# The o products of an attention kernel in tiles of 64 rows, in two banks held for a whole head group, with two visits a stretch

## The chip, the cores and the metric

One core of a Trainium2 chip. The metric is device time in microseconds of one execution. TensorE (PE) multiplies, its weight loads are shown apart as PEld; VectorE is DVE, ScalarE is ACT, GpSimd is POOL, and SyncE (SP) issues the DMAs. Matmul results land in PSUM, which has eight banks of 128 partitions x 512 fp32 values.

## The reference, cut to what matters

x is 2048 tokens x 640 channels, with 32 heads of 20 channels that share one key and one value head.

```python
q = heads(x @ wq); k = x @ wk; v = x @ wv
scores = einsum("bhqd,bkd->bhqk", q, k) * Dh ** -0.5
o = einsum("bhqk,bkd->bhqd", softmax(scores), v)
a = merge(o) @ wo
u = gelu(einsum("bsd,sf->bdf", layernorm(x), w1) + b1)   # over tokens, F = 1728
b = transpose(einsum("bdf,fs->bds", u, w2) + b2)
return g * a + (1 - g) * b                               # g = sigmoid(x . gate_w)
```

## The kernel before, in words

**Data.** Matrices are split into a high and a low part in a 32-bit type that TensorE takes in one pass; a product is then three matmuls (high x high, high x low, low x high). Most have a contraction of at most 64 rows and occupy one half of TensorE's array, 64 rows x 128 columns, so that two run side by side, one in each half. The probabilities `p` and the values `v_sb` are plain fp32, and each matmul on them shows as two passes in the trace.

**Attention.** A head group `n` is four heads by 512 queries; there are 32 (`NU`). A unit `u` is one head group and one block of 128 keys (`kb`), 512 in all. For a unit there are four scores (`qk`, line 677: two in each half of the array), each 128 keys x 512 queries for one head, in a PSUM bank of their own; ACT turns each into a tile `p` (line 686). The o product of a unit (line 788) multiplies `v_sb` (128 keys x 32 columns: 20 channels, and ones for the sum of the softmax) with each of the four `p`: four tiles of 128 rows x 32 columns, side by side, into the four quarters of one bank `o`. Row maxima are found ahead, from products of their own (`ms_next`, line 508) that DVE reduces (line 514).

**Order.** After a lead-in, a Python planner writes the order of instructions. The work is cut into 244 stretches: 84 of the first MLP layer (`b1_jobs`, line 1069), 128 of the second (`b2_jobs`, line 866) and 32 of the output projection (`a_jobs`, line 1005), whose accumulating matmuls go into one bank `g` and are called `fs` in `main`. In a stretch one half of the array runs scores and maxima (`xs`), the other the `fs` with a few scores and maxima before and after; halves change roles from stretch to stretch. `main` keeps a clock for each half (`lanes`) and a list of banks with the times at which they come free (`pool`, seven banks: three `ms`, three `s`, one `o`, which scores and maxima use too), and always writes the half that is free first. Each score or maximum counts 0.232 us (`X_US`), each of the `fs` 0.147 us (`F_US`).

At the end of each stretch comes one visit: the o products of two units in one go (`pv_group`, line 778), eight matmuls of 128 x 32 in a bank taken from `pool`. ACT copies the result out (line 797 or 800), and POOL adds it to the head group's sum (line 801); after the last block of keys the sum is scaled and stored in steps that `settle` spreads over later stretches.

Units 488 to 511 (`TAIL`) follow in blocks of their own, with the same `pv_group`, one unit at a time and summing in the bank.

Of the kernel before, what the change touches and what calls it, by code (L numbers as in the profile page):

```python
# [9 lines left out]
F32 = mybir.dt.float32  # L10
F32R = mybir.dt.float32r
AF = mybir.ActivationFunctionType
# [5 lines left out]
P = 128  # L18
S, D, H, DH, F = 2048, 640, 32, 20, 1728
NS = S // P  # L20
# [4 lines left out]
NB = 512  # L25
NQB = S // NB
NQ = H // 4
NU = NQB * NQ
PRO = 7
LEAD = 45  # L30
TAIL = 24
# [13 lines left out]
def mix_kernel(ctx: ExitStack, tc: tile.TileContext, A_x, A_wq, A_wk, A_wv, A_wo,  # L45
               B_x, B_w1, B_b1, B_w2, B_b2, gate_w, out):
    nc = tc.nc
    x = A_x[0]
# [17 lines left out]
    v_sb = const.tile([P, NS, 32], F32, name="v_sb")  # L66
# [109 lines left out]
    with tc.tile_pool(name="pa", bufs=1) as pa, \  # L176
# [236 lines left out]
        for sb in range(NQB):  # L413
# [11 lines left out]
            for m in range(DC):  # L425
# [3 lines left out]
                p = q_parts(m, ts)  # L429
# [37 lines left out]
    ev = ctx.enter_context(tc.tile_pool(name="ev", bufs=1))  # L467
# [7 lines left out]
    def bank_take():  # L475
        i = min(range(len(pool)), key=lambda j: pool[j][0])
        return pool.pop(i)[1]
# [170 lines left out]
    ptiles = {}  # L648
# [125 lines left out]

    otile, sums = [], [None]
    later = []

    def pv_group(us, keep=False):
        n, kb = units[us[0]]
        assert units[us[-1]][0] == n  # L780
        if not otile:
            otile.append(bank_take())
        o = otile[0]
        opened = not keep or kb == 0 or us[0] == len(units) - TAIL
        ends = kb + len(us) == NS
        for i, u in enumerate(us):
            for hh in range(4):
                nc.tensor.matmul(o[32 * hh:32 * hh + 32, :], v_sb[:, kb + i, :], ptiles.pop((u, hh)),  # L788
                                 start=opened and i == 0, stop=(i == len(us) - 1) and (ends or not keep),
                                 skip_group_check=True)  # L790
        if not keep:
            begin = max(clock["act"], clock["pv"] + 0.14)
            clock["act"] = begin + 0.477
            pool.append((begin + 0.65, otile.pop()))
            if kb == 0:
                sums[0] = ev.tile([P, NB], F32, name="acc", bufs=2)
                nc.scalar.activation(sums[0], o, AF.Copy)
            else:
                part = ev.tile([P, NB], F32, name="part", bufs=2)
                nc.scalar.activation(part, o, AF.Copy)  # L800
                nc.gpsimd.tensor_add(sums[0], sums[0], part)  # L801
        if ends and n < NU - 1:
            qb, g = divmod(n, NQ)
            ot = ev.tile([P, NB // 32, 32], F32, name="ot")
            rl = ev.tile([P, NB // 32], F32, name="rl")
            on = sums[0]
            flat = ot.rearrange("p c e -> p (c e)")
            oh, ol = flat.bitcast(F32R), on.bitcast(F32R)
            if keep:
                nc.vector.tensor_add(on, on, o)  # L810

            def turned():
                nc.vector.transpose(flat, on)
                nc.vector.reciprocal(rl, ot[:, :, DH])
                nc.vector.tensor_mul(ot, ot, rl[:, :, None].to_broadcast([P, NB // 32, 32]))

            def back():
                nc.vector.transpose(on, flat)

            def sums_out():  # L820
                for hh in range(4):
                    r = 32 * hh + DH
                    nc.sync.dma_start(out=l_scr[0, n, hh:hh + 1], in_=on[r:r + 1, :])

            def sums_in():
                nc.sync.dma_start(out=rl, in_=l_scr[0, n].rearrange("h (r c) -> (h r) c", r=32))

            def inverse():
                busy("dve", 0.17)
                nc.vector.reciprocal(rl, rl)  # L830
                nc.sync.dma_start(out=l_scr[1, n].rearrange("h (r c) -> (h r) c", r=32), in_=rl)

            def inverse_in():
                for hh in range(4):
                    nc.sync.dma_start(out=flat[32 * hh:32 * hh + 32, :],
                                      in_=l_scr[1, n, hh:hh + 1].to_broadcast([32, NB]))

            def scale():
                nc.gpsimd.tensor_mul(on, on, flat)

            def high():
                nc.gpsimd.tensor_copy(oh, on)

            def low():
                nc.gpsimd.tensor_sub(ol, on, f32(oh))
                for j, t in enumerate((oh, ol)):
                    for hh in range(4):
                        r = (4 * g + hh) * DH
                        nc.sync.dma_start(out=o_scr[j, r:r + DH, qb * NB:(qb + 1) * NB],
                                          in_=f32(t[32 * hh:32 * hh + DH, :]))  # L850

            first = (None, turned, back) if keep else (sums_out, sums_in, None, inverse, inverse_in, None, scale)
            later.extend((False, f) for f in (*first, high, low))
# [299 lines left out]

    lanes = [0.0, 0.0]
    fresh = [True, True]

    def issue(b, us, f, t):
        clock["now"] = max(t, clock["now"])
        f()
        lanes[b] = clock["now"] + us + (FIRST if fresh[b] else 0.0)  # L1160
        fresh[b] = False

    def main(k, vs, n_max):
        b = k % 2
        fs, rest, done = ph[k]
        fs, done = list(fs), list(done)
        known, kept = set(row_max), set(sent)
        end = 2 * ((vs[-1] if vs else -1) + 1)
        xs, side = pattern(k)
        before, after = side.split("F")  # L1170
        need = end + AHEAD - sc[b]
        if xs.count("s") < need:
            i = len(xs) * 2 // 3
            xs = xs[:i] + "s" * (need - xs.count("s")) + xs[i:]
        while xs.count("s") > need:
            i = xs.rindex("s")
            xs = xs[:i] + xs[i + 1:]
        if xs.count("m") < n_max[b]:
            xs += "m" * (n_max[b] - xs.count("m"))
        while xs.count("m") > n_max[b]:  # L1180
            i = xs.rindex("m")
            xs = xs[:i] + xs[i + 1:]
        after += "m" * (n_max[1 - b] - (before + after).count("m"))
        while (before + after).count("m") > n_max[1 - b]:
            if "m" in after:
                after = after.replace("m", "", 1)
            else:
                before = before.replace("m", "", 1)
        before = "s" * (end - sc[1 - b] - (before + after).count("s")) + before
        xs, before, after = list(xs), list(before), list(after)  # L1190
        total, count = len(xs) + len(before) + len(after) + len(fs), 0
        while fs or after or before or xs:
            if count == (total + 1) // 2:
                settle()
            count += 1
            free = min(e for e, _ in pool)
            tx = max(lanes[b], free) if xs else 1e9
            tf = 1e9
            if before or (after and not fs):
                tf = max(lanes[1 - b], free)  # L1200
            elif fs:
                tf = lanes[1 - b]
            if len(xs) == 1 and fs and not after:
                tx = 1e9
            if tf < tx or tf == tx and not before:
                if before or not fs:
                    c = (before or after).pop(0)
                    issue(1 - b, X_US, (s_next if c == "s" else ms_next)(1 - b) or (lambda: None), tf)
                else:
                    issue(1 - b, F_US, fs.pop(0), tf)  # L1210
                    while done and not fs:
                        done.pop(0)()
            else:
                c = xs.pop(0)
                issue(b, X_US, (s_next if c == "s" else ms_next)(b) or (lambda: None), tx)
        ms_done()
        spare[0] = len(row_max) == NU
        settle(len(vs) == 2)
        if vs:
            n, kb = units[vs[0]][0] + 1, units[vs[0]][1]  # L1220
            if n in kept and n in qtiles and n not in back_in:
                fetch_max(n)
                back_in.add(n)
        for f in rest:
            f()
        for i in sorted(known - sent):
            store_max(i)
            sent.add(i)
        if vs:
            start = max([max(lanes) + DRAIN, min(e for e, _ in pool)] + [ready[v] for v in vs])  # L1230
            clock["pv"] = start + len(vs) * PV_US + ENTER
            lanes[:] = [clock["pv"]] * 2
            fresh[:] = [True, True]
            pv_group(vs)

    ps_l.clear()
    in_lead.close()
# [5 lines left out]
    v = 0  # L1243
    clock.update(now=0.0, act=ACT_AT, dve=0.5, pv=0.0)
    for k in range(len(ph)):
# [5 lines left out]
        if k == len(ph) - 2:  # L1251
            w_last = split_last(raw)
    assert v == len(units) - TAIL
    spare[0] = True
    ring[:0] = extra_p

# [152 lines left out]
```

## Time and profile before

| | |
|---|---|
| median of 2 runs | 1608.35 us (1608.32 to 1608.38) |
| the profiled execution | 1608.27 us, its span 1606.5 us |
| granted TensorE clock | 1.00 |
| lead-in (projections, LayerNorm, first part of layer 1) | 0 to 161.8 us |
| 84 stretches with layer 1 | 161.8 to 662.3 us |
| 128 stretches with layer 2 | 662.3 to 1377.4 us |
| 32 stretches with the output projection | 1377.4 to 1532.2 us |
| the last 24 units and the end | 1532.2 to 1606.5 us |

The profile is one execution. A busy PE means that a matmul was under way, not that the array was full: matmuls overlap, and the distance from one start to the next says more than a duration. In a timeline row stand start, duration, engine, line, operation, output and inputs, then rows x columns of the array and the shape of the moving operand; several instructions of one kind that overlap are merged (x16).

### The profile page before, as it was taken

What the parts mean: (1) busy time and instruction counts of PE and PEld (TensorE: products, weight loads), DVE (VectorE), ACT (ScalarE), POOL (GpSimd) and SP (SyncE); (2) the same over time, 40 slices, a digit from 0 to 9 for tenths busy, and PEclk for the clock granted to TensorE, in tenths of its full rate; (3) what the DMA queues carried; (4) which work ended last, traced back from release to release, by engine and by line L of the source; (5) the groups of instructions that cost most, each with busy time, mean ns of one, the idle gap of its engine ahead of it and who ended that gap; (6) DMA issues with size and microseconds to landing.
All of it is one profiled execution on the core that took longest, in us unless ns stands there. A gap on an engine that the chain in (4) does not pass through costs nothing.

```text
span 1606.5 us, 39460 instructions
## 1 busy us (share of the span) xinstructions
PE 1600.9 (100%) x14864; PEld 1123.2 (70%) x14864; DVE 1355.0 (84%) x2301; ACT 1309.1 (81%) x2566; POOL 867.6 (54%) x976
## 2 busy tenths in 40 slices
PE   9999999999999999999999999999999999999999
PEld 7899677767776777666666666666666666666676
DVE  6689999999999999888888888888888888766644
ACT  4546888888888888888888888888888888999974
POOL 6568676768777687644544434454544333344420
PEclk9999999999999999999999999999999999999999
DMA  7655223323233323222222122222222112245521
GB/s 218 212 171 143 73 74 80 86 64 94 76 81 85 82 67 80 64 73 81 73 70 68 51 67 67 70 73 81 73 73 69 54 50 68 85 123 181 165 87 57
DMA packets 183750, 145.07 MB, mean 90 GB/s; under 512 B 38291, under 2 KB 145424, under 8 KB 183560
## 3 DMA queue, kind: packets, MB, share of 16 engines
q1 hardware_dynamic: 183272, 142.23, 31.4%
q8 instruction: 117, 1.92, 0.5%
q14 instruction: 73, 0.60, 0.1%
q10 hardware_dynamic: 288, 0.33, 0.1%
HBM read 108.75 MB, written 32.15 MB: 88 GB/s over the span
## 4 chain that ended last, share of the span: by engine, by line
PE 98%; DVE 1%; POOL 0%; ACT 0%; issue 0%; DVEq 0%; POOLq 0%
PE s L788 16%; PE ms L788 11%; PE g L866 11%; PE s L677 10%; PE g L1069 9%; PE ms L677 9%; PE ms L508 6%; PE s L508 6%; PE pp L307 4%; PE o L677 3%; PE o L508 2%; PE g L1005 2%; PE o L788 2%; PE s L720 1%; PE g L720 1%; PE s L960 1%
## 5 line engine op out<-in xcount | busy, mean ns | idle before, releaser
L514 DVE TENSOR_REDUCE mp<-ms 128x1 f32<-128x512 f32 x889 | 583.1, 682 | 79.8 <-PE ms L508 64.9
L686 ACT ACTIVATE p<-s 128x512 f32<-128x512 f32 x938 | 543.2, 617 | 39.6 <-PE ms L788 12.8
L514 DVE TENSOR_REDUCE mp<-s 128x1 f32<-128x512 f32 x759 | 503.2, 683 | 75.1 <-PE s L508 61.0
L686 ACT ACTIVATE p<-ms 128x512 f32<-128x512 f32 x808 | 471.9, 614 | 35.1 <-PE s L788 11.8
L801 POOL TENSOR_TENSOR acc<-acc,part 128x512 f32<-128x512 f32 x213 | 275.0, 1291 | 311.2 <-ACT part L800 300.8
L677 PE MATMUL s<-qst,kst 62*128 62x512 f32 x944 | 362.9, 407 | 0.0
L508 PE MATMUL ms<-kst,qmx 60*128 60x512 f32 x889 | 357.5, 416 | 0.0
L677 PE MATMUL ms<-qst,kst 62*128 62x512 f32 x810 | 319.1, 407 | 0.0
L1069 PE MATMUL g<-slot,wh 64*128 64x320 f32 x1344 | 306.1, 313 | 0.3 <-ACT p L686 0.3
L508 PE MATMUL s<-kst,qmx 60*128 60x512 f32 x759 | 304.0, 414 | 0.2 <-DVE mp L514 0.2
L788 PE MATMUL s<-p,v_sb 128*32 128x512 f32 x2240 | 269.3, 598 | 0.0
L1069 PEld LDWEIGHTS g<-slot,wh 64*128 64x128 f32 x1344 | 216.6, 185 | 70.1 <-issue 49.4
L134 POOL TENSOR_TENSOR wl<-wr,wh 128x512 fp32r<-128x512 f32 (+1 forms) x176 | 218.1, 1239 | 28.0 <-ACT wh L131 16.3
L514 DVE TENSOR_REDUCE mp<-o 128x1 f32<-128x512 f32 x308 | 210.1, 682 | 18.5 <-PE o L508 17.8
L677 PEld LDWEIGHTS s<-qst,kst 62*128 62x128 f32 x944 | 174.2, 185 | 59.1 <-ACT p L686 27.6
L1069 PE MATMUL g<-slot,wl 64*128 64x320 f32 x672 | 205.4, 306 | 0.0
L866 PE MATMUL g<-u,wh 64*128 64x320 f32 x864 | 196.5, 309 | 0.0
L866 PE MATMUL g<-slot,wh 64*128 64x320 f32 x864 | 196.4, 309 | 0.0
L677 PEld LDWEIGHTS ms<-qst,kst 62*128 62x128 f32 x810 | 150.0, 186 | 56.8 <-ACT p L686 28.3
L788 PE MATMUL ms<-p,v_sb 128*32 128x512 f32 x1560 | 189.4, 598 | 0.0
L686 ACT ACTIVATE p<-o 128x512 f32<-128x512 f32 x273 | 168.3, 617 | 12.7 <-PE ms L788 6.9
L508 PEld LDWEIGHTS ms<-kst,qmx 60*128 60x128 f32 x889 | 164.2, 185 | 3.6
(270 smaller groups left out, 3101.8 us busy)
## 6 DMA issues: line engine op xcount, KB each, us to landing
wr<-in_B_w_dram SPq DMA_DIRECT2D x136, 256.0 KB
qmx<-q_scr SPq DMA_DIRECT2D x192, 80.0 KB
qst<-q_scr SPq DMA_DIRECT2D x192, 80.0 KB
ot<-l_scr SPq DMA_DIRECT2D x120, 64.0 KB
y_scr<-yo SPq DMA_DIRECT2D x16, 320.0 KB
slot<-o_scr SPq DMA_DIRECT2D x16, 320.0 KB
o_scr<-ot SPq DMA_DIRECT2D x124, 40.0 KB
o_scr<-acc SPq DMA_DIRECT2D x124, 40.0 KB
```

What stands on the lines that cost most here:

```text
L134: nc.gpsimd.tensor_sub(wl[:, :nv], wr[:, :nv], f32(wh[:, :nv]))
L307: nc.tensor.matmul(pp, w, t, start=first and n == 0, stop=not more and n == len(steps) - 1)
L508: nc.tensor.matmul(ms, qmax[n][64 * b:64 * b + 60, pr, qt * P:(qt + 1) * P], kst[64 * b:64 * b + 60, kq * NB:(kq + 1) * NB], start=True, s ...
L514: r = nc.vector.tensor_reduce(mtiles[n][:, c, kq:kq + 1], ms, axis=AX.X, op=ALU.max)
L677: nc.tensor.matmul(s, kst[64 * b:64 * b + 62, kb * P:(kb + 1) * P], q[64 * b:64 * b + 62, pr, :], start=True, stop=True)
L686: e = nc.scalar.activation(p, s, AF.Exp, scale=SCALE)
L720: nc.tensor.matmul(pu[r][:, :HD2], w[rows, c, :], h[rows, st, :], start=(st == 0 and k == 0), stop=(st == NS - 1 and k == 2))
L788: nc.tensor.matmul(o[32 * hh:32 * hh + 32, :], v_sb[:, kb + i, :], ptiles.pop((u, hh)), start=opened and i == 0, stop=(i == len(us) - 1) a ...
L801: nc.gpsimd.tensor_add(sums[0], sums[0], part)
L866: other_tile(half, nc.tensor.matmul(hold["p"][:, :HD2], w[r, i, :], u[d][r, fc, :], start=(hold["n"] == 1), stop=(hold["n"] == 6 * FC - 3)))
L1005: other_tile(half, nc.tensor.matmul(hold["p"][:, :HD2], o[r, c, :], w[r, c, d * HD2:(d + 1) * HD2], start=(hold["n"] == 1), stop=(hold["n" ...
L1069: other_tile(half, nc.tensor.matmul(hold["p"][:, :HD2], w[r, st % HS, :], h[d][r, st, :], start=(hold["n"] == 1), stop=(hold["n"] == 6 * NS)))
```

## The change

Each o product becomes two, one for each half of the keys (64 rows x 32 columns), in the half of the array where these rows lie. Each half has an o bank of its own, which is taken at the first block of keys of a head group and given back after the last: the sum over the 16 blocks is now made in PSUM, and ACT and POOL add the two banks once (`o_out`). The four products of a unit in one half are written as two pairs (`o_pair`, `j` 0 and 1), as steps of that half's queue of work, counted 0.43 us each (`V_US`). Of the two units of a stretch, one has its place in the middle (at 0.5 of `xs`, at 0.6 of `fs`), the other at the end. The planner no longer lets both halves wait for each other around a visit. The list `waiting` stays empty. The last 24 units still use `pv_group`.

```diff
+    obank, used = {}, {}
+
+    def o_out(n, upto):
+        sums[0] = ev.tile([P, NB], F32, name="acc", bufs=2)
+        part = ev.tile([P, NB], F32, name="part", bufs=2)
+        for b, t in enumerate((sums[0], part)):
+            o = obank.pop((n, b))
+            begin = max(clock["act"], clock["now"] + 0.9)
+            clock["act"] = begin + 0.477
+            nc.scalar.activation(t, o, AF.Copy)
+            pool.append((begin + 0.65, o))
+        nc.gpsimd.tensor_add(sums[0], sums[0], part)
+        unit_end(n, upto)
+
+    def o_pair(u, b, j):
+        n, kb = units[u]
+        if (n, b) not in obank:
+            obank[n, b] = bank_take()
+        o, rows = obank[n, b], slice(64 * b, 64 * b + 64)
+        last = kb == NS - 1 or u == len(units) - TAIL - 1
+        for hh in (2 * j, 2 * j + 1):
+            nc.tensor.matmul(o[32 * hh:32 * hh + 32, :], v_sb[rows, kb, :], ptiles[u, hh][rows, :],
+                             start=kb == 0, stop=last, skip_group_check=True)
+        used[u] = used.get(u, 0) + 1
+        if used[u] == 4:
+            for hh in range(4):
+                ptiles.pop((u, hh))
+            if last:
+                o_out(n, kb + 1)
...
-        if not keep:
-            begin = max(clock["act"], clock["pv"] + 0.14)
-            clock["act"] = begin + 0.477
-            pool.append((begin + 0.65, otile.pop()))
-            if kb == 0:
-                sums[0] = ev.tile([P, NB], F32, name="acc", bufs=2)
-                nc.scalar.activation(sums[0], o, AF.Copy)
-            else:
-                part = ev.tile([P, NB], F32, name="part", bufs=2)
-                nc.scalar.activation(part, o, AF.Copy)
-                nc.gpsimd.tensor_add(sums[0], sums[0], part)
-        if ends and n < NU - 1:
+        unit_end(n, kb + len(us), keep, o)
+
+    def unit_end(n, upto, keep=False, o=None):
+        if upto == NS and n < NU - 1:
...
+    X_AT, F_AT, V_US = (0, 0.5, 1), (0, 0.6, 1), 0.43
...
+        def cut(items, places):
+            out, p = [], 0
+            for at, us in zip(places, [waiting, *([u] for u in vs)]):
+                n = round(at * len(items))
+                out += items[p:n] + [("v", (u, None, j)) for u in us for j in range(2)]
+                p = n
+            return out + items[p:]
+
+        xq = cut([("x", c) for c in xs], X_AT)
+        fq = [("x", c) for c in before] + cut([("f", f) for f in fs], F_AT) + [("x", c) for c in after]
...
+            h = 1 - b if tf < tx else b
+            kind, what = q[h].pop(0)
...
+            elif kind == "v":
+                issue(h, V_US, lambda: o_pair(what[0], h, what[2]), t)
...
-        if vs:
-            start = max([max(lanes) + DRAIN, min(e for e, _ in pool)] + [ready[v] for v in vs])
-            clock["pv"] = start + len(vs) * PV_US + ENTER
-            lanes[:] = [clock["pv"]] * 2
-            fresh[:] = [True, True]
-            pv_group(vs)
```

On TensorE, before, the end of one stretch in the second layer and the start of the next (`s`, `ms` and `o` are the rotating banks, whatever they hold; L677 scores, L508 products for maxima, L866 the layer's own matmuls, L788 o products):

```order
L866 MATMUL g<-slot_83,wh 128x320
L508 MATMUL ms<-kst,qmx 128x512
L866 MATMUL g<-slot_83,wl 128x320
L677 MATMUL s<-qst,kst 128x512
L788 MATMUL s<-p,v_sb 32x512 x8
L677 MATMUL s<-qst,kst 128x512
L508 MATMUL o<-kst,qmx 128x512
L866 MATMUL g<-slot_83,wh 128x320
```

All eight o products of two units stand together, and in the 37 rows of the stretch there is no other visit.

On TensorE, after, the middle of a stretch in the second layer (L887 is the line that was L866, L798 the new o products; `s` and `o` here are the two banks of the sums):

```order
L508 MATMUL s<-kst,qmx 128x512
L887 MATMUL g<-u_1163,wh 128x320
L798 MATMUL o<-p,v_sb 32x512 x2
L887 MATMUL g<-u_1163,wl 128x320
L798 MATMUL s<-p,v_sb 32x512 x2
L798 MATMUL o<-p,v_sb 32x512 x2
L798 MATMUL s<-p,v_sb 32x512 x2
L508 MATMUL s<-kst,qmx 128x512
L887 MATMUL g<-u_1163,wh 128x320
```

The eight products of one unit stand in the middle of the stretch, pair by pair in turn for the two halves, with one of the layer's matmuls between the first pair and the rest.

On TensorE, after, the end of the same stretch:

```order
L887 MATMUL g<-u_1163,wl 128x320
L798 MATMUL s<-p,v_sb 32x512 x2
L508 MATMUL ms<-kst,qmx 128x512
L798 MATMUL o<-p,v_sb 32x512 x2
L798 MATMUL s<-p,v_sb 32x512 x2
L798 MATMUL o<-p,v_sb 32x512 x2
L677 MATMUL ms<-qst,kst 128x512
```

The other unit's eight products, with a product for a maximum between the first pair and the rest.

More of the change, by code (lines that the diff above doesn't have):

```diff
@@ L1155, in mix_kernel @@
     fresh = [True, True]
+    waiting = []
+    X_AT, F_AT, V_US = (0, 0.5, 1), (0, 0.6, 1), 0.43
     def issue(b, us, f, t):
@@ L1189, in main, with at @@
         before = "s" * (end - sc[1 - b] - (before + after).count("s")) + before
-        xs, before, after = list(xs), list(before), list(after)
-        total, count = len(xs) + len(before) + len(after) + len(fs), 0
-        while fs or after or before or xs:
+        def cut(items, places):
[7 more added lines that the diff above has]
+        fq = [("x", c) for c in before] + cut([("f", f) for f in fs], F_AT) + [("x", c) for c in after]
+        waiting.clear()
+        q = {b: xq, 1 - b: fq}
+        n_f = len(fs)
+        total, count = len(xq) + len(fq), 0
+        def at(h):
+            if not q[h]:
+                return 1e9
+            kind, what = q[h][0]
+            if kind == "x":
+                return max(lanes[h], min(e for e, _ in pool))
+            if kind == "v":
+                u = what[0]
+                if any((u, i) not in ptiles for i in range(4)):
+                    return 1e8
+                t = max(lanes[h], ready[u] + 0.05)
+                return t if (units[u][0], h) in obank else max(t, min(e for e, _ in pool))
+            return lanes[h]
+        while xq or fq:
             if count == (total + 1) // 2:
@@ L1195, in main @@
             count += 1
[L1196 to L1203, printed above, removed]
-                tx = 1e9
[L1205 to L1212, printed above, removed]
-            else:
-                c = xs.pop(0)
-                issue(b, X_US, (s_next if c == "s" else ms_next)(b) or (lambda: None), tx)
+            tx, tf = at(b), at(1 - b)
+            if len(xq) == 1 and n_f and not after:
+                tx = 1e9
+            h = 1 - b if tf < tx else b
+            kind, what = q[h].pop(0)
+            t = min(tx, tf)
+            assert t < 1e8, (k, q)
+            if kind == "x":
+                issue(h, X_US, (s_next if what == "s" else ms_next)(h) or (lambda: None), t)
+            elif kind == "v":
+                issue(h, V_US, lambda: o_pair(what[0], h, what[2]), t)
+            else:
+                issue(h, F_US, what, t)
+                n_f -= 1
+                while done and not n_f:
+                    done.pop(0)()
         ms_done()
@@ L1253, in mix_kernel @@
     assert v == len(units) - TAIL
+    for u in waiting:
+        for j in range(2):
+            for h in range(2):
+                clock["now"] = lanes[h] = max(lanes[h], ready[u] + 0.05)
+                o_pair(u, h, j)
+                lanes[h] += V_US
+    lanes[:] = [max(lanes) + DRAIN] * 2
     spare[0] = True
```

## The prediction

> **What bounds the kernel now.** I read the page's busy times and the chain that ended last first, then the busy times of the stretches of the program, then single matmuls on TensorE's timeline.
>
> ```profile
> span 1606.5 us, 39460 instructions
> PE 1600.9 (100%) x14864; PEld 1123.2 (70%) x14864; DVE 1355.0 (84%) x2301; ACT 1309.1 (81%) x2566; POOL 867.6 (54%) x976
> ...
> PE 98%; DVE 1%; POOL 0%; ACT 0%; issue 0%; DVEq 0%; POOLq 0%
> ...
> 161.80:662.30 500.50, 500.50 (x4789) 355.13 (x4792) 464.42 (x791) 420.88 (x823) 366.59 (x432) 1.00 0.31 80
> 662.30:1377.40 715.10, 715.10 (x6686) 478.64 (x6685) 631.28 (x1073) 611.12 (x1186) 321.07 (x347) 1.00 0.23 68
> 1377.40:1532.20 154.80, 154.80 (x1425) 98.97 (x1424) 101.57 (x172) 150.19 (x305) 66.24 (x69) 1.00 0.46 139
> ```
>
> The last three rows are the part that the change rewrites, with the columns us, PE, PEld, DVE, ACT, POOL, clock, DMA: 84 stretches of MLP layer 1 (5.96 us each), 128 of layer 2 (5.59) and 32 of the output projection (4.84). PE has no gap in any of them, the granted clock is 1.00, and 98% of the chain is PE. So time here is TensorE's, and what counts is how matmuls follow each other. One end of a stretch:
>
> ```profile
> 701.05 0.43 PE L677 MATMUL s<-qst,kst 62*128 62x512 f32 x1
> 701.42 1.92 PE L788 MATMUL s<-p,v_sb 128*32 128x512 f32 x16
> 703.27 0.50 PE L677 MATMUL s<-qst,kst 62*128 62x512 f32 x1
> 703.27 0.50 PE L508 MATMUL o<-kst,qmx 60*128 60x512 f32 x1
> 703.61 0.31 PE L866 MATMUL g<-u,wh 64*128 64x320 f32 x1
> 703.61 0.39 PE L508 MATMUL ms<-kst,qmx 60*128 60x512 f32 x1
> 703.76 0.30 PE L866 MATMUL g<-u,wh 64*128 64x320 f32 x1
> 703.84 0.39 PE L677 MATMUL ms<-qst,kst 62*128 62x512 f32 x1
> ...
> 701.42 0.16 PEld L788 LDWEIGHTS s<-p,v_sb 128*32 128x32 f32 x8 [0.25 <-DVE mp L514]
> 701.87 0.13 PEld L788 LDWEIGHTS s<-p,v_sb 128*32 128x32 f32 x4 [0.30 <-issue]
> 702.30 0.13 PEld L788 LDWEIGHTS s<-p,v_sb 128*32 128x32 f32 x4 [0.30 <-issue]
> ...
> 702.73 0.61 PE L788 MATMUL s<-p,v_sb 128*32 128x512 f32 x4
> ```
>
> Scores (L677) and row-maximum products (L508) fill 64 rows by 128 columns of the array, one half each. In a running stream the next one of a half starts 0.23 us after the last (703.61 to 703.84) although each takes 0.39: they overlap. Around the o products (L788, 128 rows by 32 columns) the overlap is gone. They start 0.37 after the last score, 0.14 more than 0.23. Their 16 passes run in four rounds of four, about 0.43 apart. The next score starts 0.54 after the last round, when that is nearly done (0.61), and the score after it another 0.34 later, 0.11 more than usual. A visit of two units costs 0.14 + 1.85 + 0.11 = 2.10 us, and 244 of them 512 us.
>
> Is it the type of number or the shape of the tile that stops the overlap? The trace has both cases apart:
>
> ```profile
> 40.18 1.04 PE L299 MATMUL pt<-ident,xa 128*128 128x128 f32 x8
> 40.97 1.18 PE L307 MATMUL pp<-slot,wq_hi 128*128 128x512 f32 x4
> ...
> 94.83 0.40 PE L307 MATMUL pp<-xT_lo,wq_hi 128*128 128x512 f32 x1
> 95.06 0.40 PE L307 MATMUL pp<-qmx,wq_lo 128*128 128x512 f32 x1
> 95.39 0.56 PE L720 MATMUL s<-slot,wh 64*128 64x320 f32 x4
> ...
> 94.83 0.19 PEld L307 LDWEIGHTS pp<-qmx,wq_lo 128*128 128x128 f32 x1
> 95.39 0.30 PEld L720 LDWEIGHTS s<-slot,wh 64*128 64x128 f32 x4 [0.37 <-issue]
> ```
>
> At 40.97 plain fp32 transposes are followed by split products, same shape: the product starts before the transposes end (41.22). At 95.39 the shape goes from 128x128 to 64x128: the matmul starts 0.33 after the one before instead of 0.23, and even its weights, usually loaded a step ahead (94.83), wait until then. So a change of shape waits for the array to run empty; a change of type doesn't.
>
> **The change, part by part.** (a) Each o product is cut into two, of 64 rows by 32 columns, so a unit has eight instead of four. Stream time doesn't depend on the rows (0.23 us from 94.83 to 95.06 with 128 rows, 0.23 with 62 to 64), so the array needs the same two rounds of 0.43 us a unit if all eight tiles run side by side. Issue isn't in the way: the eight loads from 701.42 on took 0.16 us in all.
>
> (b) Shapes now alternate more often. What stands on TensorE in the built programs: 244 visits before; 488 after, one unit each, of which 179 are eight o products in a row, 197 are cut 2 + 6 and 110 cut 2 + 4 + 2 (two more into 2 + 2 + 4 and 2 + 2 + 2 + 2) by matmuls of 128 columns that the planner puts between: 910 runs of o products and 422 gaps inside visits (401 of one matmul, 20 of two, one of three).
>
> (c) If a change of shape empties the array as at 95.39 and 701.42, a run pays its time in full. One run has two rounds: 0.45 (701.42 to 701.87) + 0.54 (702.73 to 703.27) = 0.99 us. 488 visits x (0.14 + 0.11) = 122 us, 910 x 0.99 = 901 us. A matmul caught between two runs starts without weights loaded (0.50 instead of 0.39), and the next run can begin when it is nearly done: 0.37 + 0.11 - 0.04 = 0.44 for 512 columns (0.04 since the score at 701.05 was late itself, 0.43), about 0.35 for a g product, which is 0.08 shorter (0.31 against 0.39); it does work that had to be done, half of 0.23 since it fills one of two halves. That leaves 0.32 or 0.28, say 0.31; x 422 = 131 us. Together 1154 us where 512 stood: +642 us.
>
> (d) The sums of two banks a unit go out once, not once a visit: 244 ACT copies become 62, and 213 additions on POOL 31.
>
> ```profile
> L801 POOL TENSOR_TENSOR acc<-acc,part 128x512 f32<-128x512 f32 x213 | 275.0, 1291 | 311.2 <-ACT part L800 300.8
> L800 ACT ACTIVATE part<-s 128x512 f32<-128x512 f32 x121 | 72.4, 598 | 75.0 <-PE s L788 66.1 <-POOL acc L801 2.7 <-DVE mm L549 2.4
> ```
>
> 182 x 0.60 = 109 us of ACT and 182 x 1.29 = 235 us of POOL go. PE waits for neither now (it is busy all the time), so I put this at nothing. The copies that stay, two of them after the last o product of a head group, hold ACT's queue with the exponentials behind them for about the 1 us that the products take, 31 times: 0 to 31 us, at nothing while PE is late.
>
> (e) Two of the seven rotating banks are held for a whole head group; scores and maxima have five. With PE slowed by (c) to 8.2 us and more a stretch, DVE's 5.5 us of work (464.42 / 84) and ACT's 5.0 (420.88 / 84) leave room: nothing. Without (c) this is what decides, below.
>
> Sum: 1606.5 + 642 = 2248.5 us of span, and the 1.8 us that this run's time (1608.27) had over its span: **2250 us**. The median of the runs, 1608.35, is the same time within 0.1. Bounds for this case: a run can't be shorter than its streams, 0.86 (910 x 0.13 = 118 less), and the gaps may be dearer, up to the 0.99 a lone matmul would take were it as slow as a run (about 100 more with odd waits): 2130 to 2350.
>
> By the Trainium skill, TensorEngine Tiling (Array Packing), section Key Properties, a switch of tiling mode drains the engine, and 64x128 and 64x32 are listed as different modes; by that rule the sum is the one above. The rows agree where the number of rows changes (0.33 and 0.37 instead of 0.23); no row of before has 64x32 beside 64x128.
>
> **The rivals.** *No emptying where both shapes have 64 rows.* Every wait in the trace is at a change between 128 and 64 rows, where the new tile overlaps all that runs. An o product in the upper half touches nothing of a score in the lower half, so the two may overlap as two scores do. Then a visit costs its streams, 4 x 0.43 = 1.72 us for two units instead of 2.10: 244 x 0.38 = 93 us less, 1515 us. It decides as soon as the matmuls in the gaps cost no more than their own 0.23. What would give some back is DVE and the banks:
>
> ```profile
> 700.06 0.68 DVE L514 TENSOR_REDUCE mp<-ms 128x1 f32<-128x512 f32 x1
> 700.66 0.68 DVE L514 TENSOR_REDUCE mp<-s 128x1 f32<-128x512 f32 x1
> 701.26 0.68 DVE L514 TENSOR_REDUCE mp<-o 128x1 f32<-128x512 f32 x1
> ```
>
> Maxima follow each other every 0.60 us; the first part has about 9 a stretch, 5.4 of what would be 5.96 - 0.38 = 5.58 us. With five banks PE can't run ahead far enough to hide every delay, so I expect a third back: **1545 us**, from 1515 to 1620.
>
> The Trainium skill, TensorE: Matmul & The Clock Gate, Part 3, describes overlap as a matter of each sub-array: a load may pass a running matmul when its row group differs. By that, scores of one half would run on beside o products of the other and the time would be this rival's; the two loads of different halves at 703.27 agree, but they are of one shape.
>
> *Each half empties by itself.* A half waits only for its own matmuls. Each unit then costs each half 0.14 + 0.99 + 0.11 = 1.24 us, two 2.48 against 2.10: 244 x 0.38 = +93, **1700 us**, and up to 1850 if the queue, which is in order, holds the other half back for part of the 422 gaps (422 x 0.35 = 148).
>
> *The change doesn't do what it says:* the planner could have laid the two halves' o products one after the other; the order speaks against it, since they stand next to each other or with one or two matmuls between.
>
> **How the numbers follow.** Emptying at every change of shape: 0.52, since all three kinds of change in the trace do it (128x128 to 64x128, 64x128 to 128x32 and back). No emptying: 0.36. Each half for itself: 0.12. A measurement of this kernel tells about 2% (32 us) from no change. Of the 0.36, 0.25 lies below 1576, 0.08 within 2%, 0.03 above; the other two are slower. So faster 0.25, same 0.08, slower 0.67. Likeliest 2250, with its own range 2130 to 2350. For 8 in 10 the range has to take in most of the other cases as well: 1535 to 2350, which leaves out the better third of the no-emptying case and little above.
>
> **What would show it.** Right: stretches of 8 to 9 us; after each run of L798 a pause like that at 703.27, with the weights of both halves loaded only then, and lone scores of 0.50 us between two runs; DVE and ACT near 60%. Wrong: scores starting 0.23 apart in one half while L798 records run in the other, stretches near 5.6 us, DVE over 90% in the first part and PE waiting for banks. The half-by-half case shows stretches near 6 us with a pause in one half alone.

## The result, and the profile after

The changed kernel took 2333.39 us (median of 2 runs, 2333.37 to 2333.41) against 1608.35: 1.451 times as long, interval 1.4446 to 1.457. The forecast was 2250, in a range of 1535 to 2350; the case that it took for the likeliest, the array runs empty at every change of shape, is the one that came.

The page of after, its busy times and the chain, and the windows over the rewritten parts (us, PE, PEld, DVE, ACT, POOL, clock, DMA):

```profile
span 2331.4 us, 46743 instructions
PE 2323.5 (100%) x18768; PEld 1206.9 (52%) x18768; DVE 1398.3 (60%) x2301; ACT 1288.0 (55%) x2384; POOL 637.0 (27%) x794
...
PE 99%; DVE 1%; ACT 0%; issue 0%; POOL 0%; DVEq 0%; ACTq 0%; POOLq 0%
...
159.70:919.00 759.30, 759.07 (x6106) 376.19 (x6110) 473.18 (x785) 411.29 (x754) 286.05 (x364) 1.00 0.21 53
919.00:2021.00 1102.00, 1100.07 (x8743) 532.64 (x8745) 661.35 (x1074) 597.67 (x1091) 201.55 (x256) 1.00 0.15 44
2021.00:2252.00 231.00, 230.83 (x1935) 105.83 (x1935) 105.59 (x172) 149.68 (x280) 35.42 (x44) 1.00 0.31 95
```

PE is again almost never idle and the clock is 1.00, yet the 84, 128 and 32 stretches take 759, 1102 and 231 us instead of 501, 715 and 155: together 722 of the 725 us. A stretch of the first part went from 5.96 to 9.04 us. DVE does the same work as before in more time, ACT the same but for 182 copies, and the share of PEld fell from 70% to 52%: its 1207 us, 1123 before, are spread over a longer span. A busy PE here is one on which matmuls wait for each other.

One visit of after that is cut 2 + 4 + 2, on TensorE's timeline, and below it the weight loads of the same time:

```profile
1255.41 0.39 PE L508 MATMUL s<-kst,qmx 60*128 60x512 f32 x1
1255.50 0.30 PE L887 MATMUL g<-slot,wl 64*128 64x320 f32 x1
1255.73 1.05 PE L798 MATMUL s<-p,v_sb 64*32 64x512 f32 x4
1256.71 0.50 PE L677 MATMUL ms<-qst,kst 62*128 62x512 f32 x1
1257.05 0.40 PE L508 MATMUL ms<-kst,qmx 60*128 60x512 f32 x1
1257.38 0.62 PE L798 MATMUL s<-p,v_sb 64*32 64x512 f32 x2
...
1258.37 0.50 PE L677 MATMUL o<-qst,kst 62*128 62x512 f32 x1
1258.80 0.62 PE L798 MATMUL ms<-p,v_sb 64*32 64x512 f32 x2
...
1255.73 0.14 PEld L798 LDWEIGHTS s<-p,v_sb 64*32 64x32 f32 x4 [0.19 <-issue]
1256.71 0.18 PEld L677 LDWEIGHTS ms<-qst,kst 62*128 62x128 f32 x1 [0.84 <-ACT p L686]
1257.37 0.11 PEld L798 LDWEIGHTS s<-p,v_sb 64*32 64x32 f32 x2 [0.37 <-issue]
```

From 1255.73 to 1256.71 two o products, a quarter of the array, are all that runs, once the matmuls begun before them have ended. The score at 1256.71 lies in the other half; neither it nor its weights start before the o products have run out. At 1258.37 a single score has the array to itself for 0.43 us. Over all 910 runs of o products in the trace, the time from the first start to the next other matmul's is 0.98 us on average for two products, 0.99 for four, 1.01 for six and 1.04 for eight: two cost as much as eight. From a lone matmul's start to the next run it is 0.34 us (320 columns, 65 times) or 0.43 (512 columns, 336 times).

### The profile page after: what moved, and what is told of

It is laid out like the page before. It is cut to its first block, busy times and chain, and to the rows that moved or that the text cites. A ratio compares the mean times of both kernels' runs of the same rounds, so it can differ in the third digit from the quotient of the medians.

```text
span 2331.4 us, 46743 instructions
## 1 busy us (share of the span) xinstructions
PE 2323.5 (100%) x18768; PEld 1206.9 (52%) x18768; DVE 1398.3 (60%) x2301; ACT 1288.0 (55%) x2384; POOL 637.0 (27%) x794
## 4 chain that ended last, share of the span: by engine, by line
PE 99%; DVE 1%; ACT 0%; issue 0%; POOL 0%; DVEq 0%; ACTq 0%; POOLq 0%
PE ms L798 18%; PE s L798 15%; PE g L887 8%; PE s L677 8%; PE ms L677 7%; PE s L508 7%; PE ms L508 7%; PE g L1090 6%; PE o L798 6%; PE pp L307 3%; PE o L677 3%; PE o L508 2%; PE g L1026 2%; PE s L720 2%; PE ms L817 1%; PE s L981 0%
## 5 line engine op out<-in xcount | busy, mean ns | idle before, releaser
L514 DVE TENSOR_REDUCE mp<-s 128x1 f32<-128x512 f32 x862 | 575.0, 684 | 367.6 <-PE s L508 261.7
L514 DVE TENSOR_REDUCE mp<-ms 128x1 f32<-128x512 f32 x822 | 548.9, 685 | 368.8 <-PE ms L508 268.5
L798 PE MATMUL ms<-p,v_sb 64*32 64x512 f32 x3584 | 576.6, 601 | 0.1
L798 PE MATMUL s<-p,v_sb 64*32 64x512 f32 x3008 | 529.0, 601 | 0.1
L677 PE MATMUL s<-qst,kst 62*128 62x512 f32 x916 | 379.2, 428 | 0.1
L508 PE MATMUL s<-kst,qmx 60*128 60x512 f32 x862 | 370.7, 442 | 1.2 <-DVE mp L514 0.3
L508 PE MATMUL ms<-kst,qmx 60*128 60x512 f32 x822 | 353.5, 441 | 0.4
L677 PE MATMUL ms<-qst,kst 62*128 62x512 f32 x832 | 346.6, 428 | 0.2
L1090 PE MATMUL g<-slot,wh 64*128 64x320 f32 x1344 | 337.6, 326 | 0.0
L677 PEld LDWEIGHTS s<-qst,kst 62*128 62x128 f32 x916 | 166.0, 184 | 168.0 <-DVE mp L514 79.7
L508 PEld LDWEIGHTS s<-kst,qmx 60*128 60x128 f32 x862 | 157.8, 185 | 164.5 <-ACT p L686 76.5
L788 POOL TENSOR_TENSOR acc<-acc,part 128x512 f32<-128x512 f32 x31 | 39.8, 1284 | 720.0 <-ACT part L786 718.0
L508 PEld LDWEIGHTS ms<-kst,qmx 60*128 60x128 f32 x822 | 150.4, 185 | 158.4 <-ACT p L686 76.5
L677 PEld LDWEIGHTS ms<-qst,kst 62*128 62x128 f32 x832 | 151.3, 185 | 148.0 <-DVE mp L514 76.0
L798 PE MATMUL o<-p,v_sb 64*32 64x512 f32 x1216 | 225.3, 601 | 0.0
L887 PE MATMUL g<-slot,wh 64*128 64x320 f32 x864 | 224.2, 327 | 0.0
```

The costliest lines, as they stand in the source:

```text
L508: nc.tensor.matmul(ms, qmax[n][64 * b:64 * b + 60, pr, qt * P:(qt + 1) * P], kst[64 * b:64 * b + 60, kq * NB:(kq + 1) * NB], start=True, s ...
L514: r = nc.vector.tensor_reduce(mtiles[n][:, c, kq:kq + 1], ms, axis=AX.X, op=ALU.max)
L677: nc.tensor.matmul(s, kst[64 * b:64 * b + 62, kb * P:(kb + 1) * P], q[64 * b:64 * b + 62, pr, :], start=True, stop=True)
L798: nc.tensor.matmul(o[32 * hh:32 * hh + 32, :], v_sb[rows, kb, :], ptiles[u, hh][rows, :], start=kb == 0, stop=last, skip_group_check=True)
L887: other_tile(half, nc.tensor.matmul(hold["p"][:, :HD2], w[r, i, :], u[d][r, fc, :], start=(hold["n"] == 1), stop=(hold["n"] == 6 * FC - 3)))
L1090: other_tile(half, nc.tensor.matmul(hold["p"][:, :HD2], w[r, st % HS, :], h[d][r, st, :], start=(hold["n"] == 1), stop=(hold["n"] == 6 * NS)))
```

## The experiments

Two groups: spare matmuls in the kernel before, which measure one change of shape by itself, and versions of the two kernels that take the change apart. Where no interval is given, the altered kernel was executed once.

**spare_128, spare_32, spare_64.** The kernel before with one more matmul ahead of a score; 32 or 64 instead of 128 columns in the other two:

```diff
+        if not ps_l and pr == 0 and b == 0 and kb % 2 == 0 and u < len(units) - TAIL:
+            nc.tensor.matmul(s[:128, :], kst[:62, kb * P:kb * P + 128], q[:62, pr, :], start=True, stop=True)
         nc.tensor.matmul(s, kst[64 * b:64 * b + 62, kb * P:(kb + 1) * P], q[64 * b:64 * b + 62, pr, :],
```

> The kernel before, with one spare product ahead of the first score of every second unit (244 in all), 62 rows x 128 columns in the first half of the array, into the score's own bank, which the score then overwrites: extra work of the usual shape. All theories: 244 x 0.12 to 0.23 us = 29 to 57 us more, 1637 to 1665 us.

> The same spare product with 32 columns instead of 128 (same rows, same 512 moving columns, same half, same type). Theory A, the array empties at every change of shape, also where both shapes have 64 rows: 0.14 before it, about 0.43 for it alone, 0.11 behind it, 244 x 0.68 = 166 us more, about 1775 us, and the other half's matmuls stand still meanwhile. Rival B, tiles of 64 rows run on beside each other whatever their columns: as with 128 columns, 1637 to 1665 us. Rival C, each half empties by itself: about 0.14 + 0.23 + 0.11 in one half, which is not always the later one: 1665 to 1725 us, with the other half's matmuls 0.15 or 0.23 apart as ever.

> The same spare product with 64 columns. If any change of columns empties the array, as with 32 columns, about 1775 us; if only tiles of 32 columns do so, 1637 to 1665 us.

Measured, beside 1607.46 of the kernel before: 1645.00, 1641.66 and 1641.34 us. Theory A as written here fell: 32 columns cost no more than 128. The timeline of spare_32 (L678 is the spare product, L679 the score behind it):

```profile
762.48 0.39 PE L679 MATMUL ms<-qst,kst 62*128 62x512 f32 x1
762.54 0.31 PE L868 MATMUL g<-slot,wh 64*128 64x320 f32 x1
762.69 0.39 PE L868 MATMUL g<-slot,wl 64*128 64x320 f32 x1
762.72 0.44 PE L508 MATMUL ms<-kst,qmx 60*128 60x512 f32 x1
762.92 0.39 PE L678 MATMUL ms<-qst,kst 62*32 62x512 f32 x1
763.15 0.39 PE L679 MATMUL ms<-qst,kst 62*128 62x512 f32 x1
```

From spare product to score it is 0.23 us, as between any two. The profile calls its shape 62*32, but that is the number of columns it uses. The traces don't show which of the four groups of 32 columns an instruction claims; the built programs do:

| instruction | type | uses | claims |
|---|---|---|---|
| scores, maxima, layers | split | 128 columns | all four groups |
| spare_32, spare_64 | split | 32, 64 | all four |
| o products | plain fp32 | 32 | one |
| plain_128, plain_64, plain_32 (below) | plain fp32 | 128, 64, 32 | four, two, one |

So these runs had changed neither claim nor type, and the next three are plain fp32, the first with all four groups claimed, the other two with fewer.

**plain_128, plain_64, plain_32.** The same spare product with both operands read as plain fp32 (128 columns shown):

```diff
+            nc.tensor.matmul(s, f32(kst[:62, kb * P:(kb + 1) * P]), f32(q[:62, pr, :]), start=True, stop=True)
```

> The spare products of the runs before were in the split type, and the built instruction of that type claims all 128 columns of the array whatever it uses; so those with 32 and 64 columns changed no shape. Here the spare product is plain fp32 (two passes), 62 rows x 128 columns: another type, the same claim. Theory A2, the array empties where the claimed shape changes: no emptying here, only two passes of extra work in one half, 244 x 0.22 to 0.45 = 54 to 110 us more, 1660 to 1717 us. Rival E, plain fp32 beside the split type empties the array, whatever the shape: 244 x (0.14 + 0.99 + 0.11) = 303 us more, about 1910 us.

> The same in plain fp32 with 64 columns, where the instruction claims only the first 64. A2: as with 32 columns, about 1910 us. If only claims of 32 columns empty the array: 1660 to 1717 us. E: about 1910 us.

> The same in plain fp32 with 32 columns, where the instruction claims only the first 32: the shape and type of the change's o products. A2 and E: 244 x 1.24 = 303 us more, about 1910 us, and the matmuls of the other half stand still. Rival B, tiles of 64 rows run on beside each other: 1660 to 1717 us.

Measured, beside 1608.30: 1796.89, 1894.09 and 1888.02 us. Claims of 64 and 32 columns cost 286 and 280 us, near the 303 of A2 (and of E). The 128 columns cost 189, more than expected, as I had counted the two passes at 0.22 to 0.45 us. They are 0.43 each and fill their half for 0.86: 244 x 0.86 = 210 at most. What tells the theories apart is the other half of the array. First plain_128, then plain_32 (L678 the spare product, L1071 layer 1 in the other half):

```profile
496.00 0.30 PE L1071 MATMUL g<-slot,wh 64*128 64x320 f32 x1
496.09 0.59 PE L678 MATMUL ms<-qst,kst 62*128 62x512 f32 x1
496.15 0.31 PE L1071 MATMUL g<-slot,wl 64*128 64x320 f32 x1
496.30 0.45 PE L1071 MATMUL g<-slot,wh 64*128 64x320 f32 x2
496.52 0.59 PE L678 MATMUL ms<-qst,kst 62*128 62x512 f32 x1
496.55 0.79 PE L679 MATMUL ms<-qst,kst 62*128 62x512 f32 x1
496.59 0.35 PE L1071 MATMUL g<-slot,wl 64*128 64x320 f32 x1
```

```profile
512.94 0.31 PE L1071 MATMUL g<-slot,wh 64*128 64x320 f32 x1
513.17 1.04 PE L678 MATMUL ms<-qst,kst 62*32 62x512 f32 x2
514.15 0.50 PE L679 MATMUL ms<-qst,kst 62*128 62x512 f32 x1
514.15 0.41 PE L1071 MATMUL g<-slot,wl 64*128 64x320 f32 x1
```

Beside the plain product of 128 columns the other half goes on at 0.15 us a matmul. Beside the one of 32 columns it stands still from 512.94 to 514.15, and both halves start again together. It does so every time: in plain_32 and plain_64 no other matmul starts for 0.97 and 1.00 us behind any of the 244 spare products. That clears the type by itself (rival E) and rules out the halves emptying separately and 64-row tiles running on (rivals C and B): what empties the whole array is a change in the columns claimed. No split product that claims fewer than all four groups was run, so the rule is shown for plain fp32 tiles among split ones.

**whole_runs.** The changed kernel; a half whose o products are due waits for the other half, and the eight go out in one run:

```diff
             if kind == "v":
                 u = what[0]
...
-                t = max(lanes[h], ready[u] + 0.05)
+                o = q[1 - h][0]
+                if o[0] != "v" or o[1][0] != u:
+                    return 1e7
+                t = max(*lanes, ready[u] + 0.05)
...
-                issue(h, V_US, lambda: o_pair(what[0], h, what[2]), t)
+                for hh in range(2):
+                    while q[hh] and q[hh][0][0] == "v" and q[hh][0][1][0] == what[0]:
+                        q[hh].pop(0)
+                clock["now"] = t
+                for j in range(2):
+                    for hh in range(2):
+                        o_pair(what[0], hh, j)
+                lanes[:] = [t + 2 * V_US] * 2
```

> The changed kernel with the eight o products of a unit always written in one run, two visits a stretch as before: 488 runs instead of 910, and no gaps. Theory A: 422 runs of 0.98 us and the gaps' 130 us go: 2333 - 414 - 130 = about 1790 us. Rival D, the time comes from the five banks or from the tiles of 64 rows as such, which are the same here: 2250 us or more.

Measured: 1830.89 us beside 1607.46. 502 of the 725 us went with the cutting of the visits, and rival D fell, though 41 us fewer went than the 1790 expected. 223 us remain with 488 whole visits.

**one_visit and five_banks.** one_visit is whole_runs with both units at the stretch's end; five_banks is the kernel before with two banks taken out of rotation, and given back for the last 24 units:

```diff
-    X_AT, F_AT, V_US = (0, 0.5, 1), (0, 0.6, 1), 0.43
+    X_AT, F_AT, V_US = (0, 1, 1), (0, 1, 1), 0.43
```

```diff
-    pool.extend(zip(FREE_AT, tiles))
+    spared, tiles = tiles[1:3], tiles[:1] + tiles[3:]
+    pool.extend(zip(FREE_AT[:1] + FREE_AT[3:], tiles))
```

> The changed kernel with all sixteen o products of a stretch's two units in one run at its end: 244 runs of four rounds, as before the change, but in tiles of 64 rows and with two banks held, so that five rotate. Theory A: what is left of the 725 us is only what five banks cost, 1608 to 1690 us. Rival D (tiles of 64 rows are slow as such, or don't run side by side): 1900 us or more.

> The kernel before with five rotating banks instead of seven, o taken from among them, otherwise the same. If five banks explain the 83 us by which the change was dearer than forecast: the same price or more here, where a stretch has one visit to catch up in instead of two, 1640 to 1750 us. If the price is only that the two halves are out of step at twice as many visits: 1608, within 2%.

Measured, beside 1607.76: one_visit 1827.51 us (1.1366, interval 1.1349 to 1.1383), five_banks 1836.98 (1.1424, 1.1405 to 1.1443). Both are far over what was expected, and within 10 us of each other. In the traces the 243 visits of one_visit that another follows take 1.88 us each, where those of before take 1.85; the loss lies between the visits, where no o product stands: 1126 us there (five_banks 1146, before 918). So tiles of 64 rows cost next to nothing as such, and two banks fewer cost 229 us with one visit a stretch, in the order that the planner writes for five. The two cases aren't quite alike: in five_banks each visit also takes one of the five, and one_visit has fewer copies and additions. In five_banks, the scores and maxima of the last 2 us before a visit (the layer's matmuls left out), the reductions, and one weight load:

```profile
803.94 0.40 PE L508 MATMUL s<-kst,qmx 60*128 60x512 f32 x1
804.19 0.50 PE L508 MATMUL s<-kst,qmx 60*128 60x512 f32 x1
804.53 0.45 PE L677 MATMUL ms<-qst,kst 62*128 62x512 f32 x1
804.83 0.46 PE L677 MATMUL o<-qst,kst 62*128 62x512 f32 x1
804.98 0.49 PE L508 MATMUL s<-kst,qmx 60*128 60x512 f32 x1
805.39 0.49 PE L677 MATMUL s<-qst,kst 62*128 62x512 f32 x1
805.72 0.44 PE L508 MATMUL ms<-kst,qmx 60*128 60x512 f32 x1
806.09 1.92 PE L788 MATMUL s<-p,v_sb 128*32 128x512 f32 x16
...
804.65 1.88 DVE L514 TENSOR_REDUCE mp<-s 128x1 f32<-128x512 f32 x3
...
805.39 0.18 PEld L677 LDWEIGHTS s<-qst,kst 62*128 62x128 f32 x1 [0.23 <-DVE mp L514]
```

Scores and maxima start 0.15 to 0.41 us apart here, most over 0.23, while DVE reduces without a pause, and the load at 805.39 waits for a reduction. Between the visits of five_banks 484 weight loads stood idle for over 0.15 us until a reduction or an exponential, which give banks back, had ended, 148 us in all; before, 33 did, 7 us. So with five banks PE can't run ahead, and waits for DVE and ACT once the banks are full.

**one_shape and less_room.** The changed kernel with every tile of a stretch in one claimed shape:

```diff
+    vst = ev.tile([P, 96 + NS * P], F32R, name="vst")
+    nc.gpsimd.memset(f32(vst), 0.0)
+    nc.gpsimd.tensor_copy(vst[:, 96:].rearrange("p (n c) -> p n c", c=P)[:, :, :32], v_sb)
...
-            nc.tensor.matmul(o[32 * hh:32 * hh + 32, :], v_sb[rows, kb, :], ptiles[u, hh][rows, :],
-                             start=kb == 0, stop=last, skip_group_check=True)
+            at = 96 + kb * P - 32 * hh
+            nc.tensor.matmul(o, vst[rows, at:at + P], ptiles[u, hh].bitcast(F32R)[rows, :],
+                             start=kb == 0 and hh == 0, stop=last and hh == 3, skip_group_check=True)
```

less_room is the kernel before with 11 p tiles (`NP`) and three raw weight tiles (`w1r`).

> The changed kernel with its o products in the split type (the probabilities and v rounded to the high part alone, which leaves their low parts out), one pass each, the 32 columns of v padded with zeros to 128 at the head's place, so that the four heads of a unit add up in the same bank: every matmul of a stretch then claims 64 rows x 128 columns. To make room: 11 p tiles instead of 12, three raw weight tiles instead of four, one part tile. Order and banks are as in the changed kernel. A2: no emptying, an o product costs 0.23 us as any other, 4 x 0.23 a unit in each half; 2.23 us of visit and ends become 1.86, 1520 us, plus what five banks cost with two visits a stretch (0.1 to 0.5 us): 1520 to 1640 us. Rival D, the places of the o products in the stretch or the banks make the change slow: over 1900 us.

> The kernel before with 11 p tiles instead of 12 and three raw weight tiles instead of four, the room that one_shape had to give up. If the 1676 us of one_shape are the price of five banks: 1608, within 1%. If they are the price of that room: 1650 us or more.

Measured: one_shape 1676.19 us beside 1608.30 (1.0422, interval 1.0392 to 1.0453); less_room 1639.96 beside 1608.28. The timeline of one_shape (L802 the o products, L680 scores, L891 layer 2):

```profile
903.81 0.31 PE L891 MATMUL g<-slot,wh 64*128 64x320 f32 x1
903.94 0.39 PE L802 MATMUL s<-p,vst 64*128 64x512 f32 x1
903.96 0.31 PE L891 MATMUL g<-slot,wl 64*128 64x320 f32 x1
904.11 1.08 PE L802 MATMUL s<-p,vst 64*128 64x512 f32 x7
904.88 0.39 PE L511 MATMUL ms<-kst,qmx 60*128 60x512 f32 x1
905.03 0.31 PE L891 MATMUL g<-slot,wh 64*128 64x320 f32 x1
```

With nearly the same order (each pair counts 0.464 us instead of 0.43) and the same banks, 657 of the 725 us are gone: the o products run in 0.94 us (903.94 to 904.88) without a pause on either side. That is the change as it was meant, and it is still slower than before. Of the 156 us between the 1520 that streams alone would give and 1676, 32 are the room given up (less_room, which came out between its two forecasts), if the two prices add up; the other 124 I put down to the five banks, after five_banks. That is not shown: there is no version with seven, for which PSUM has no room. None of the versions run beats the kernel before.

## Why the prediction was right

- **What bounds.** The reading that time is TensorE's, and that starts count rather than busy time, held: busy shares stayed at 100% while the time went up by 45%.
- **The emptying, 0.52.** Right, and now shown where the trace of before couldn't show it: at 1255.73 and in plain_32 a change in one half stops the other. The argument had a gap: it spoke of the shape of the tile, and by spare_32 and the plain products it is the shape that the instruction claims. The change's o products claim what they use, so the forecast wasn't hurt.
- **By the Trainium skill,** TensorEngine Tiling (Array Packing), section Key Properties, a switch of tiling mode drains the engine; the runs agree (no other matmul starts for 0.97 us in plain_32 and 1.00 in plain_64), with the addition that a split-type tile of 32 columns is not another mode (0.23 us to the next in spare_32). The overlap of loads with running matmuls that the Trainium skill, TensorE: Matmul & The Clock Gate, Part 3, allows when row groups differ was not seen across a change of the claimed shape: at 1256.71 the load for the other half came only when the o products had nearly run out.
- **Price of a run,** forecast 0.99: measured 0.98 to 1.04. 910 runs: 423 x 0.979 + 111 x 0.992 + 197 x 1.006 + 179 x 1.036 = 908 us, forecast 901.
- **Price of a gap,** forecast 0.35 and 0.44: measured 0.34 and 0.43; 65 x 0.34 + 336 x 0.43 + 20 x 0.65 + 0.6 = 180 us, of which 422 x 0.11 = 48 was work to be done anyway: 132, forecast 131.
- **Time between visits, the term that was too small.** "488 visits x (0.14 + 0.11)" was set against 244 x 0.25: 61 us more. Counting in the trace, stretch by stretch, the time between visits less the mean of the two halves' work (0.232 and 0.147 us a matmul), an end costs (914.1 - 822.2) / 243 = 0.38 us before and (1005.9 - 775.3) / 487 = 0.47 after, 139 us more. That is the 78 us that the sum lacked, nearly all of the 83 between 2250 and 2333. Had an end kept the price that it really had before, 0.38 and not the 0.25 read off one visit, 32 of the 78 would be there (244 x 0.13): ends were undersized, perhaps because the two halves don't finish together. The other 44 (487 x 0.09) came with the change.
- **Five banks, put at nothing** because PE would be late. That step failed, by up to the 78 us. DVE and ACT are indeed at 60% and 55%, but over a whole stretch; between two visits PE still waits for them. In after:

```profile
345.05 1.08 ACT L686 ACTIVATE p<-s 128x512 f32<-128x512 f32 x2 [2.47 <-PE s L677]
345.27 0.31 PE L1090 MATMUL g<-slot,wh 64*128 64x320 f32 x1
345.33 0.40 PE L508 MATMUL ms<-kst,qmx 60*128 60x512 f32 x1
345.70 0.18 PEld L508 LDWEIGHTS s<-kst,qmx 60*128 60x128 f32 x1 [0.39 <-ACT p L686]
345.70 0.50 PE L508 MATMUL s<-kst,qmx 60*128 60x512 f32 x1
345.71 0.42 PE L1090 MATMUL g<-slot,wh 64*128 64x320 f32 x1
```

The load at 345.70 waits until the first of two exponentials has ended (0.60 us from 345.05) and gives its bank back, and both halves pause. Between the visits of after 273 loads waited so for ACT or DVE, over 0.15 us each and 76 us in all; before, 33 did, 7 us. The 69 us between are of the size of what the sum lacked, but idle time of loads isn't the same as lost time: how the 78 divide between ends and banks stays open.
- **The range held partly by luck.** Its top, 2350, allowed 100 us for dearer gaps. The gaps cost what was forecast; what filled the allowance was the time between visits.
- **Copies and additions, put at nothing.** 182 additions on POOL fell away (L788 x31 for L801 x213), and its busy time went from 868 to 637 us; what that did to the time wasn't measured by itself. ACT lost as many copies, but its busy time fell by 21 us only (1309 to 1288), not 109: two exponentials in a row take 1.08 us together, one alone 0.60, and 1067 of the 2048 now start with ACT free, 299 before.

```profile
L788 POOL TENSOR_TENSOR acc<-acc,part 128x512 f32<-128x512 f32 x31 | 39.8, 1284 | 720.0 <-ACT part L786 718.0 <-PE ms L677 2.0
```

- **The no-emptying rival** was priced at 1515 to 1620 us. one_shape gives 1676, or about 1644 without the room it lost: its streams ran as the rival had them, and if the rest is the banks' price, they would have taken back more than the gain, not a third.

## What to carry to other kernels

Before tiles of different shapes are mixed on TensorE, look in the trace for one change of shape and take the time from the last matmul's start to the first of the other shape: if it is near the full duration (0.33 and 0.37 of some 0.40 us here) and not the usual step (0.23), count that at every change, for both halves of the array, and keep like shapes together. What counts is the columns that an instruction claims, which need not be those that the profile shows it using. And a bank kept for a sum is a bank that no score can use: find out what fewer rotating banks cost alone, by taking them from the old kernel, before building on it.

## What was unexpected of the hardware

A split-type tile of 62 x 32 ran between tiles of 128 columns at the usual 0.23 us (spare_32), while a plain fp32 tile of the same size emptied the array (plain_32: 280 us for 244 of them, 1.15 us each, of which the same product with 128 columns, which empties nothing, costs 0.77). And two of seven rotating banks were worth 229 us, 14%, in a kernel whose TensorE shows as 98% busy or more with either number.
